# Block-sparse attention with a softplus FFN: the turned attention rows move one piece later, and the first key loads change queue

## The chip, the cores and the metric

One core of one Trainium2 chip runs the whole program. The metric is the device time of one execution in microseconds. Before the change three runs gave 786.46, 788.22 and 792.05 us; the median is 788.22 us.

## The reference

Attention over 4 batches of 8 heads, 768 positions in 24 blocks of 32, head size 64, float32. A query block sees its own block and both neighbours, the first and the last block, and three sampled blocks; the first and last query blocks see everything. Then a feed-forward layer on 3072 rows of 512, with 2048 hidden columns.

```python
scores = scale * np.matmul(q, k.transpose(0, 1, 3, 2))
mask = np.abs(blk_i - blk_j) <= window
mask = mask | (blk_i == 0) | (blk_j == 0) | (blk_i == n_blocks - 1) | (blk_j == n_blocks - 1)
...
attn = attn / (np.sum(attn, axis=-1, keepdims=True) + 1e-09)
...
h = x @ w_in
g = np.maximum(h, 0.0) + np.log1p(np.exp(-np.abs(h)))
return (g @ w_out).astype(np.float32)
```

## The kernel before

**Sets and units.** The 88 inner query blocks go in 22 sets ("s") of four; four more sets ("w") hold the first and last query blocks. A set has two units, each with half of the heads. For a unit, `scores` (L577) multiplies queries `qc` by gathered keys `kg` into PSUM tiles `s`; VectorE adds the mask and takes the maximum (L602, tile `pr`); `exponents` (L636) is ScalarE's exponential (L651), which also sums rows into `sums`; `transposes` (L655) turns `pr` on TensorE into PSUM tile `t` (L664), which ScalarE (L669) or VectorE (L667) copies to `pt`; `values` (L674) multiplies `pt` by the gathered values `vg` into PSUM tile `x` (L700).

**The end of a set.** `normalise` (L721) divides on VectorE: L731 and L732 invert the sums, L733 writes `xs`. `turn` (L753) transposes `xs` on TensorE into a PSUM tile `y` (L759, four matmuls); `x_high` (L770) copies it on ScalarE (L772), `x_low` (L774) takes the remainder on VectorE (L776). Both parts go into `X`, the FFN's input for three sets ("a tile", 8 in all).

**FFN, first part.** For each of 8 tiles and 6 of 16 column blocks, `hidden` (L255, tile `h`, 12 matmuls) and, three steps later, `project` (L318, tile `o`, 9 matmuls). The other ten column blocks come after attention, in a second part from about 440 us on (L1093 to L1215). Weights are converted on ScalarE and VectorE in small ticks between these (L181 to L231, tiles `raw`, `wt`, `w`).

**Who goes when.** `pieces` (L783) cuts attention into pieces. For an "s" set m the first holds its scores, the values and `normalise` of the set before; the second and third hold the transposes of its two units, with `turned_` (turn and `x_high`) and `lowered` (`x_low`) of the set before. `between` (L939) is called in the middle of `hidden`, between the products of `project` and after half steps, and runs the pieces due by then, so that FFN products stand between them. A tile's `hidden` may only be written after the third piece of its last set. In blocks under `manual_schedule`, and for SyncE everywhere, an engine follows program order. Elsewhere the framework's planner gives each engine its order from program order and from modelled costs; a later instruction may be put ahead of one that is not ready in the model. On the chip each engine then keeps that order. PSUM has four banks for `s`, `t`, `h` and `y` together (L126), and a bank is taken again once its readers are done.

**The start.** L403 loads a table of sampled blocks, broadcast to 128 partitions, from ScalarE's queue; `make_index` (L418) makes from it the rows that POOL gathers (L563). L406 loads the same blocks plain, for the registers that address key copies. Keys of batch 0 (`kT`) come in two loads, blocks 0 to 10 from SyncE and 11 to 23 from ScalarE. `gather_keys` (L500) fills `kg`: a copy of three neighbours for all four blocks (L515), the first and last block (L524), and three sampled blocks for each (L537). For the first set these copies are on VectorE and ScalarE. Meanwhile L860 keeps TensorE running with products that nobody reads (`warm`).

Of the kernel before, what the change touches and what calls it, by code (L numbers as in the profile page):

```python
# [10 lines left out]
I32 = mybir.dt.int32  # L11
# [25 lines left out]

PARK = 8

WARM = 41  # L40

AHEAD = 0.5

# [11 lines left out]
def sparse_attention_ffn(  # L55
# [344 lines left out]
                    nc.vector.memset(mask[i * BLOCK : (i + 1) * BLOCK, j, slot : slot + 1], NEG)  # L400

    def load_blocks():
        nc.scalar.dma_start(  # L403
            out=table, in_=picks.bitcast(I32).unsqueeze(1).to_broadcast([NI, BLOCK, 2 * NW])
        )
        nc.sync.dma_start(out=plain, in_=blocks.bitcast(I32).rearrange("a b -> (a b)").unsqueeze(0))  # L406

    def pack_blocks():

# [14 lines left out]
                out=ix[:, b], in0=rx, scalar1=float(BLOCK), scalar2=iof[:, b : b + 1], op0=ALU.mult, op1=ALU.add  # L424
            )

    def make_mask():

        nc.vector.tensor_tensor(
            out=tmp, in0=rp, in1=iuf.unsqueeze(2).to_broadcast([P, PG, NR]), op=ALU.subtract  # L430
        )
        nc.vector.tensor_tensor(out=tmp, in0=tmp, in1=tmp, op=ALU.mult)
        nc.vector.tensor_single_scalar(out=hit, in_=tmp, scalar=1.0, op=ALU.is_le)
        for end in (0.0, float(LAST)):
            nc.vector.scalar_tensor_tensor(
                out=hit, in0=rp, scalar=end, in1=hit, op0=ALU.is_equal, op1=ALU.max
            )
        for s in range(1, NR):

            n = NR - s  # L440
            nc.vector.tensor_tensor(out=tmp[:, :, 0:n], in0=rp[:, :, s:NR], in1=rp[:, :, 0:n], op=ALU.is_equal)
            nc.vector.tensor_tensor(out=hit[:, :, s:NR], in0=hit[:, :, s:NR], in1=tmp[:, :, 0:n], op=ALU.max)
        nc.vector.tensor_single_scalar(out=mask[:, :, 4 : 4 + NR], in_=hit, scalar=NEG, op=ALU.mult)
# [56 lines left out]
    def gather_keys(j, b, lo, hi):  # L500
        kd = kg[j % 2]
        blk0 = group[j][lo][1]

        stale = [i for i in range(lo, hi) if ended_in.get((j % 2, i)) != b]
        for i in stale:
            ended_in[j % 2, i] = b

        def of_block(i):

            eng = (nc.vector if i < 2 else nc.scalar) if j == 0 else nc.gpsimd  # L510
            copy = nc.scalar.copy if j == 0 and i >= 2 else eng.tensor_copy
            if i == lo:
                at = kT[b][:, blk0 - 1 : blk0 - 1 + NR, :]
                pattern = [list(x) for x in at.ap]
                ins = nc.vector.tensor_copy(  # L515
                    out=kd[:, lo:hi, 0:NR, :].rearrange("p i s f -> p i (s f)"),
                    in_=bass.AP(at.tensor, at.offset, [pattern[0], [NP * BLOCK, hi - lo], [1, NR * NP * BLOCK]]),
                )
                tc.keep_in_program_order(ins)
                if stale:  # L520
                    rows = slice(stale[0], stale[-1] + 1)
                    first = nc.vector.tensor_copy if j == 0 else nc.scalar.copy
                    for end, slot, blkno in ((first, NR, 0), (nc.scalar.copy, 2 * NR + 1, LAST)):
                        ins = end(  # L524
                            out=kd[:, rows, slot, :],
                            in_=kT[b][:, blkno : blkno + 1, :].to_broadcast([P, len(stale), NP * BLOCK]),
                        )
                        if j:
                            tc.keep_in_program_order(ins)
            blk = group[j][i][1] - 1  # L530
            (r,) = registers(eng, [blk // 2])
            for s in range(NR):
                x = nc.s_assert_within(
                    eng.snap((r >> (16 * (blk % 2) + 5 * s)) & 31), 0, LAST,
                    skip_runtime_bounds_check_because="a sampled block is one of the key blocks",
                )
                copy(  # L537
                    out=kd[:, i, 1 + NR + s, :], in_=kT[b][:, bass.ds(x, 1), :].rearrange("p n f -> p (n f)")
                )

        key_work.extend((j, lambda i=i: of_block(i)) for i in range(lo, hi))


# [239 lines left out]
    def pieces():  # L783

        out = []

        def piece(*fs, wide=False):
            out.append((fs, wide))

        def scored(n):  # L790
            scores(n)
            m, a = units[n]
            what, j = sets[m]
            if a < NA - 1:
                return
            if what == "s":
                load_keys(j + 2)
            elif j + 1 < B:

                gathered(key_work, NM)  # L800
                for part in (0, 3, 1, 2):
                    load_kT(j + 1, part)
                waiting.append(BEHIND)

        def valued(n):
            values(n)
            m, a = units[n]
            if a == NA - 1:
                load_values(m + 2)

        def turned_(m):
            if turns_now(m):
                turn(m)
                x_high(m)

        def lowered(m):
            if turns_now(m):
                x_low(m)

        piece((transposes, 1))  # L820
        for m in range(1, len(sets) + 1):
            u, before = 2 * m, m - 1
            kind = sets[m][0] if m < len(sets) else None
            whole = sets[before][0] == "w"
            if whole:
                piece((valued, u - 2), (transposes, u - 1))
            gone = [(valued, u - 1)] if whole else [(valued, u - 2), (valued, u - 1)]
            if kind == "s":
                piece((scored, u), (scored, u + 1), *gone, (load_queries, m + 2), (exponents, u), (normalise, before), wide=True)
                piece((exponents, u + 1), (turned_, before), (transposes, u))  # L830
                piece((lowered, before), (transposes, u + 1))
            elif kind == "w":
                piece((scored, u), (exponents, u))
                piece((scored, u + 1), *gone, (load_queries, m + 2), (exponents, u + 1), (normalise, before))
                piece((turned_, before), (transposes, u))
                out[-1] = (out[-1][0] + ((lowered, before),), False)
            else:
                piece(*gone, (normalise, before))
                piece((turned_, before))
                piece((lowered, before))  # L840
            ready[before] = len(out)
        return out
# [8 lines left out]
    weights = Weights(early + later, 3, 4)  # L851

    load_blocks()
    load_queries(0)

    load_part(0, 0, FIRST, nc.sync)
    load_part(0, FIRST, NB, nc.scalar)
    warm = ps_s.tile([P, 4, P], F32, tag="s", name="warm")
    for n in range(WARM):
        nc.tensor.matmul(warm[:, n % 4], ident, ident, start=True, stop=True)  # L860
    with tc.manual_schedule(engines={mybir.EngineType.DVE}):
        make_index()
        pack_blocks()
        make_mask()
        load_keys(0)
        gathered(key_work, 0)
    load_queries(1)
    load_values(0)
    load_keys(1)
# [584 lines left out]
```

## Time and profile before

| what | value |
|---|---|
| median of three runs | 788.22 us |
| the profiled execution | 791.96 us, span 790.2 us |
| TensorE busy | 740.5 us, 94% of the span |
| VectorE busy | 591.9 us, 75% |
| ScalarE busy | 556.5 us, 70% |
| GpSimd (POOL) busy | 270.1 us, 34% |
| mean granted TensorE clock | 0.981 |

The span runs from the first to the last instruction; 1.8 us of the execution lie around it. PE is TensorE's matmul row, PEld its weight loads, DVE VectorE, ACT ScalarE, POOL GpSimd, SP SyncE. Matmul records overlap, since matmuls are pipelined, so the start of the next record says more than the length of one. A float32 product counts as two records, a transpose as one.

### The profile page before, as it was taken

The numbers are of one execution on the slowest core, as the hardware profiler recorded it, in microseconds if no ns is written. First come the engines' busy times: TensorE is split into PE (matmuls) and PEld (weight loads), VectorE is DVE, ScalarE is ACT, GpSimd is POOL, SyncE is SP. The second block draws the span as 40 slices with busy tenths as digits, with TensorE's granted clock in tenths as the row PEclk, the third lists the DMA queues.
The fourth block names the chain that finished last, engine by engine and source line by source line (L and its number), as shares of the span: only waits on it lengthen the run. The fifth ranks groups of instructions, "written<-read, shape, count | busy, mean of one in ns | idle before, by whom it ended". The sixth has DMA issues, their size and how long they took to land.

```text
span 790.2 us, 21936 instructions
## 1 busy us (share of the span) xinstructions
PE 740.5 (94%) x8350; PEld 628.5 (80%) x8350; DVE 591.9 (75%) x1446; ACT 556.5 (70%) x1297; POOL 270.1 (34%) x446
## 2 busy tenths in 40 slices
PE   8888898899888998998999998999999999999997
PEld 7556677778777777876788977898999998989996
DVE  5689998767867867775567975677786676777865
ACT  4678987767867777777577868766667666676663
POOL 7744545315333153442010036862503413310000
PEclk9899999999999998999999999999999999999999
DMA  8788865949747698447554624302331132120301
GB/s 307 258 289 337 318 255 190 338 162 377 261 165 260 219 359 293 149 136 280 189 193 159 223 85 149 107 30 79 108 107 52 56 107 98 42 76 1 107 1 54
DMA packets 54336, 137.81 MB, mean 174 GB/s; under 512 B 5781, under 2 KB 18582, under 8 KB 50518
## 3 DMA queue, kind: packets, MB, share of 16 engines
q1 hardware_dynamic: 46466, 111.49, 40.0%
q0 software_dynamic: 7120, 23.34, 7.8%
q8 instruction: 66, 1.08, 0.5%
q10 hardware_dynamic: 644, 1.57, 0.5%
q14 instruction: 40, 0.33, 0.1%
HBM read 105.97 MB, written 30.41 MB: 173 GB/s over the span
## 4 chain that ended last, share of the span: by engine, by line
PE 69%; ACT 13%; DVE 10%; issue 3%; DMA 2%; POOL 1%; SPq 0%; POOLq 0%; ACTq 0%; DVEq 0%
PE o L1213 6%; PE o L1214 6%; PE o L1215 6%; ACT pr L651 5%; PE t L664 5%; PE a L1101 3%; PE a L1103 3%; PE a L1102 3%; PE s L596 3%; PE h L263 3%; PE h L264 3%; PE h L265 3%; PE o L327 3%; PE o L328 3%; PE o L329 3%
## 5 line engine op out<-in xcount | busy, mean ns | idle before, releaser
L563 POOL DMA_INDIRECT vg<-in_v_dram,ix x88 | 94.0, 1068 | 116.7 <-PE x L700 90.7
L651 ACT ACTIVATE pr<-pr,nmax 128x256 f32<-128x256 f32 (+1 forms) x192 | 101.8, 532 | 28.3 <-DVE nmax L602 22.8
L537 POOL COPY kg<-kT 128x128 f32 x252 | 71.7, 324 | 110.7 <-PE s L596 104.5
L1213 PE MATMUL o<-w,gh 128*128 128x512 f32 x240 | 94.4, 393 | 0.0
L1214 PE MATMUL o<-w,gh 128*128 128x512 f32 x240 | 94.3, 393 | 0.0
L1215 PE MATMUL o<-w,gl 128*128 128x512 f32 x240 | 94.0, 392 | 0.0
L1188 ACT CAST gh<-a 128x512 fp32r<-128x512 f32 x30 | 17.6, 587 | 79.1 <-DVE a L1184 79.1
L263 PE MATMUL h<-x,w 128*128 128x384 f32 x192 | 70.2, 366 | 3.2 <-issue 1.9
L602 DVE CUSTOM_DVE_ANT_1 pr<-s,mask 128x256 f32<-128x256 f32 x176 | 62.8, 421 | 8.6 <-PE s L596 8.4
L264 PE MATMUL h<-x,w 128*128 128x384 f32 x192 | 66.0, 344 | 0.0
L664 PE MATMUL t<-ident,pr 128*128 128x128 f32 x448 | 63.9, 289 | 2.2 <-ACT pr L651 0.9
L265 PE MATMUL h<-x,w 128*128 128x384 f32 x192 | 65.7, 342 | 0.0
L664 PEld LDWEIGHTS t<-ident,pr 128*128 128x128 f32 x448 | 54.2, 148 | 8.8 <-issue 2.3
L700 PEld LDWEIGHTS x<-vg,pt 128*32 128x32 f32 x2816 | 42.1, 110 | 22.9 <-issue 21.7
L327 PE MATMUL o<-w,gh 128*128 128x512 f32 x144 | 59.2, 411 | 0.0
L329 PE MATMUL o<-w,gl 128*128 128x512 f32 x144 | 57.5, 399 | 0.0
L328 PE MATMUL o<-w,gh 128*128 128x512 f32 x144 | 57.3, 398 | 0.0
L700 PE MATMUL x<-vg,pt 128*32 128x64 f32 x2816 | 48.4, 221 | 8.5 <-issue 8.5
L596 PE MATMUL s<-kg,qc 64*32 64x256 f32 x1408 | 54.3, 397 | 2.0 <-DVE pt L667 0.7
L1215 PEld LDWEIGHTS o<-w,gl 128*128 128x128 f32 x240 | 45.1, 188 | 10.1
L669 ACT COPY pt<-t 128x512 f32<-128x512 f32 x82 | 45.8, 585 | 9.5 <-PE t L664 5.3
L1172 DVE SCALAR_TENSOR_TENSOR b<-b,e 128x512 f32<-128x512 f32 x30 | 20.9, 698 | 39.9 <-ACT l L1168 39.9
(206 smaller groups left out, 2160.5 us busy)
## 6 DMA issues: line engine op xcount, KB each, us to landing
vg<-in_near_dram SPq DMA_DIRECT2D x21, 1024.0 KB
xD<-x SPq DMA_DIRECT2D x8, 1536.0 KB
raw<-in_w_in_dram SPq DMA_DIRECT2D x16, 512.0 KB
raw<-in_w_out_dram SPq DMA_DIRECT2D x16, 512.0 KB
q<-xD SPq DMA_DIRECT2D x16, 512.0 KB
vg<-in_v_dram SPq DMA_DIRECT2D x12, 512.0 KB
yD<-os SPq DMA_DIRECT2D x24, 256.0 KB
y<-yD SPq DMA_DIRECT2D x24, 256.0 KB
```

What stands on the lines that cost most here:

```text
L263: nc.tensor.matmul(out_, wh[:, cols], hi, start=(c == 0), stop=False)
L264: nc.tensor.matmul(out_, wh[:, cols], lo, start=False, stop=False)
L265: nc.tensor.matmul(out_, wl[:, cols], hi, start=False, stop=(c == NC - 1))
L327: nc.tensor.matmul(po[m], gh[:, cols], wh, start=first, stop=False)
L329: nc.tensor.matmul(po[m], gl[:, cols], wh, start=False, stop=last)
L563: nc.gpsimd.indirect_dma_start(out=vd[:, 1, i, :], out_offset=None, in_=v, in_offset=bass.IndirectOffsetOnAxis(ap=ix[:, b, blk_ : blk_ + 1 ...
L651: nc.scalar.activation(x, x, AF.Exp, bias=nmax[:, r, j : j + 1], scale=-1.0, accum_out=rs[:, h : h + 1])
L664: nc.tensor.transpose(ps[:, i], st["pr"][r][:, c * P : (c + 1) * P], ident)
L700: nc.tensor.matmul(xq[rows, h * D : (h + 1) * D], pt[r, 2 * j + c][:, rows], vd[:, c, i, h * D : (h + 1) * D], start=(c == 0), stop=(c == 1),)
L1213: nc.tensor.matmul(po[m], gh[:, cols], wh, start=first, stop=False)
L1214: nc.tensor.matmul(po[m], gh[:, cols], wl, start=False, stop=False)
L1215: nc.tensor.matmul(po[m], gl[:, cols], wh, start=False, stop=last)
```

## The change

1. In an "s" set, `turned_` of the set before leaves the second piece and goes to the head of the third, ahead of the second unit's transposes; `lowered` goes behind them. "w" sets keep their order.
2. At the start SyncE issues the table, then both loads of keys, then the first queries; ScalarE issues the plain blocks alone. Before, SyncE issued plain blocks, queries, first keys, and ScalarE the table and the second keys.
3. The first set's copy of three neighbours moves from VectorE to ScalarE and, with the copies of the end blocks, ahead of the first part of the mask (`near_mask`); the second part (`twice_mask`) comes behind VectorE's copies of sampled blocks.
4. 28 warm products instead of 41.

```diff
-WARM = 41
+WARM = 28
...
-        nc.scalar.dma_start(
+        nc.sync.dma_start(
             out=table, in_=picks.bitcast(I32).unsqueeze(1).to_broadcast([NI, BLOCK, 2 * NW])
         )
-        nc.sync.dma_start(out=plain, in_=blocks.bitcast(I32).rearrange("a b -> (a b)").unsqueeze(0))
+        nc.scalar.dma_start(out=plain, in_=blocks.bitcast(I32).rearrange("a b -> (a b)").unsqueeze(0))
...
+        def beside():
+
+            at = kT[b][:, blk0 - 1 : blk0 - 1 + NR, :]
+            pattern = [list(x) for x in at.ap]
+            ins = (nc.vector.tensor_copy if j else nc.scalar.copy)(
+                out=kd[:, lo:hi, 0:NR, :].rearrange("p i s f -> p i (s f)"),
+                in_=bass.AP(at.tensor, at.offset, [pattern[0], [NP * BLOCK, hi - lo], [1, NR * NP * BLOCK]]),
+            )
+            tc.keep_in_program_order(ins)
...
+                    if j or slot > NR:
+                        tc.keep_in_program_order(ins)
...
+            if i == lo and j:
+                beside()
...
+        if j == 0:
+            key_work.append((j, beside))
...
-                piece((exponents, u + 1), (turned_, before), (transposes, u))
-                piece((lowered, before), (transposes, u + 1))
+                piece((exponents, u + 1), (transposes, u))
+                piece((turned_, before), (transposes, u + 1), (lowered, before))
...
     load_blocks()
+    load_part(0, 0, FIRST, nc.sync)
+    load_part(0, FIRST, NB, nc.sync)
     load_queries(0)
-
-    load_part(0, 0, FIRST, nc.sync)
-    load_part(0, FIRST, NB, nc.scalar)
...
         make_index()
         pack_blocks()
-        make_mask()
         load_keys(0)
+        key_work.pop(0)[1]()
+        near_mask()
         gathered(key_work, 0)
+        twice_mask()
```

## Rows read from the trace of the kernel before

**Rows 1.** The page's head and its first part: span, then busy time of each engine, share of the span, instructions.

```profile
span 790.2 us, 21936 instructions
PE 740.5 (94%) x8350; PEld 628.5 (80%) x8350; DVE 591.9 (75%) x1446; ACT 556.5 (70%) x1297; POOL 270.1 (34%) x446
```

**Rows 2.** Busy time by stretch: the stretch in us, its length, then busy time and instructions of PE, PEld, DVE, ACT and POOL, the granted TensorE clock (1.00 is 2.4 GHz), the DMA engines' share and GB/s.

```profile
56.00:110.00 54.00, 48.59 (x842) 36.37 (x842) 51.50 (x145) 46.93 (x122) 27.17 (x56) 0.97 0.86 327
110.00:440.00 330.00, 305.57 (x4608) 254.48 (x4607) 246.97 (x678) 243.97 (x614) 103.34 (x213) 0.97 0.65 234
440.00:790.00 350.00, 340.50 (x2087) 304.18 (x2085) 254.10 (x488) 230.70 (x465) 100.78 (x84) 1.00 0.24 78
```

**Rows 3.** Waits of PE from 110 to 440 us: line, what ended the wait, then us in total, times, the longest.

```profile
PE y L759 <- DVE xs L733: 16.1, 9, 2.3
PE x L700 <- issue: 3.2, 3, 1.9
...
PE y L759 <- DVE wt L212: 1.9, 1, 1.9
```

**Rows 4.** The same view from 20 to 56 us, and (second row) from 56 to 110 us.

```profile
PE y L759 <- DVE xs L733: 3.9, 3, 1.6
...
PE y L759 <- DVE xs L733: 0.9, 1, 0.9
```

**Rows 5.** PE in order of time, one set from its scores to the next set's: start, duration, engine, line, operation, operands, count, and in brackets the idle time before with its releaser.

```profile
219.15 1.96 PE L596 MATMUL s<-kg,qc 64*32 64x256 f32 x64
...
223.93 0.34 PE L265 MATMUL h<-x,w 128*128 128x384 f32 x1
226.58 0.65 PE L759 MATMUL y<-ident,xs 128*128 128x128 f32 x4 [2.31 <-DVE xs L733]
...
228.67 0.52 PE L264 MATMUL h<-x,w 128*128 128x384 f32 x1
...
232.67 1.04 PE L664 MATMUL t<-ident,pr 128*128 128x128 f32 x8
...
237.82 1.96 PE L596 MATMUL s<-kg,qc 64*32 64x256 f32 x64
```

**Rows 6.** The same set on ACT (the fourth of eight exponentials, and the end of the eighth) and on DVE.

```profile
222.97 0.49 ACT L651 ACTIVATE pr<-pr,nmax 128x256 f32<-128x256 f32 x1
...
225.34 0.18 ACT L651 ACTIVATION_READ_ACCUMULATOR pr<-pr,nmax 128x1 f32 x1
225.56 0.17 DVE L731 TENSOR_SCALAR sums<-sums 128x8 f32<-128x8 f32 x1 [1.71 <-ACT pr L651]
...
225.88 0.64 DVE L733 TENSOR_TENSOR xs<-x,sums 128x512 f32<-128x512 f32 x1
...
227.88 0.69 DVE L776 TENSOR_TENSOR x<-y,x 128x512 fp32r<-128x512 f32 x1 [0.49 <-ACT x L772]
```

**Rows 7.** The last such wait of the stretch: ACT's fourth exponential of the set, and PE's wait.

```profile
372.41 0.49 ACT L651 ACTIVATE pr<-pr,nmax 128x256 f32<-128x256 f32 x1
...
376.02 0.66 PE L759 MATMUL y<-ident,xs 128*128 128x128 f32 x4 [2.30 <-DVE xs L733]
```

**Rows 8.** Busy time by stretch, as in rows 2: the wait of rows 5 and what follows it, then two more stretches at the low clock.

```profile
224.27:226.58 2.31, 0.00 (x1) 0.01 (x1) 0.99 (x4) 1.25 (x6) 1.54 (x4) 1.00 0.83 326
227.60:230.80 3.20, 3.20 (x13) 3.10 (x12) 2.84 (x5) 1.55 (x4) 2.14 (x2) 0.50 1.03 409
...
309.50:316.20 6.70, 5.85 (x22) 5.46 (x23) 4.27 (x9) 3.28 (x8) 2.44 (x3) 0.50 0.89 345
340.20:343.50 3.30, 3.30 (x15) 3.30 (x16) 2.37 (x5) 1.76 (x6) 2.41 (x3) 0.50 0.99 350
```

**Rows 9.** PE at the start, in order of time: the last 17 warm records, both units' scores, and the first values.

```profile
10.80 2.06 PE L860 MATMUL warm<-ident 128*128 128x128 f32 x17
12.79 2.03 PE L596 MATMUL s<-kg,qc 64*32 64x256 f32 x64
...
18.02 0.30 PE L700 MATMUL x<-vg,pt 128*32 128x64 f32 x2 [0.55 <-issue]
19.40 0.42 PE L700 MATMUL x<-vg,pt 128*32 128x64 f32 x2 [1.08 <-issue]
```

**Rows 10.** The other engines at the start: the table's issue, its user, ACT's and DVE's key copies, POOL's fourth gather of values.

```profile
0.78 1.20 ACTq L403 DMA_DIRECT2D xe<-in_picks_dram  x1
5.49 0.72 DVE L423 TENSOR_SCALAR ix<-xe,iof 128x24 int32<-128x24 int32 x4 [1.83 <-DMA xe<-in_picks_dram]
...
10.21 0.95 POOL L563 DMA_INDIRECT vg<-in_v_dram,ix  x1 [0.30 <-issue]
10.38 0.62 ACT L524 COPY kg<-kT 128x512 f32<-128x512 f32 x1 [8.35 <-DMA kT<-in_k_dram]
11.39 1.45 ACT L537 COPY kg<-kT 128x128 f32 x6 [0.40 <-DVE kg L537]
```

**Rows 11.** DMA queues from 12 to 14 us: packets, MB, share of 16 engines (q1 is SyncE's, q0 POOL's).

```profile
q1 hardware_dynamic: 95, 0.58, 71.9%
q0 software_dynamic: 88, 0.27, 34.5%
```

**Rows 12.** The last turn before the FFN's first tile, and VectorE's remainder of it.

```profile
51.63 0.65 PE L759 MATMUL y<-ident,xs 128*128 128x128 f32 x4 [0.82 <-DVE xs L733]
...
54.54 0.68 DVE L776 TENSOR_TENSOR x<-y,x 128x512 fp32r<-128x512 f32 x1
```

More of the change, by code (lines that the diff above doesn't have):

```diff
@@ L425, in make_index, with near_mask @@
             )
-    def make_mask():
+    def near_mask():
         nc.vector.tensor_tensor(
@@ L437, in make_mask, with twice_mask @@
             )
+    def twice_mask():
         for s in range(1, NR):
@@ L506, in gather_keys @@
             ended_in[j % 2, i] = b
+        def beside():
[6 more added lines that the diff above has]
+            tc.keep_in_program_order(ins)
+            if stale:
+                rows = slice(stale[0], stale[-1] + 1)
+                first = nc.vector.tensor_copy if j == 0 else nc.scalar.copy
+                for end, slot, blkno in ((first, NR, 0), (nc.scalar.copy, 2 * NR + 1, LAST)):
+                    ins = end(
+                        out=kd[:, rows, slot, :],
+                        in_=kT[b][:, blkno : blkno + 1, :].to_broadcast([P, len(stale), NP * BLOCK]),
+                    )
+                    if j or slot > NR:
+                        tc.keep_in_program_order(ins)
         def of_block(i):
@@ L511, in of_block @@
             copy = nc.scalar.copy if j == 0 and i >= 2 else eng.tensor_copy
[L512 to L529, printed above, removed]
+            if i == lo and j:
+                beside()
             blk = group[j][i][1] - 1
@@ L834, in pieces @@
                 piece((scored, u + 1), *gone, (load_queries, m + 2), (exponents, u + 1), (normalise, before))
-                piece((turned_, before), (transposes, u))
-                out[-1] = (out[-1][0] + ((lowered, before),), False)
+                piece((turned_, before), (transposes, u), (lowered, before))
             else:
```

## The prediction

> **What bounds the kernel now.** I read the page's busy shares first: TensorE works 94% of the span, nobody else over 75% [rows 1]. Then busy time by stretch. From 440 us on TensorE has 340.5 of 350 us, and the change touches nothing there. From 110 to 440 us it has 305.6 of 330, so 24.4 us are idle, while VectorE and ScalarE are busy 75% and 74%. From 56 to 110 us VectorE is busy 51.5 of 54 us: that stretch is VectorE's [rows 2]. Then PE's waits: of the 24.4 us, 16.1 and 1.9 are one wait, ten times over, that of the turn `y` for `xs`; the next one is 3.2 us [rows 3]. Nothing stands beside it: in one such case PE has no work for 2.31 us [rows 5, 8].
>
> Why is `xs` late? In that set scores begin at 219.15 and `hidden`'s first half ends at 224.27. L731, which inverts the sums of a later set, stands ahead of L733 on VectorE and waits until the eighth exponential is read out at 225.52; then L733 ends at 226.52 and `y` starts [rows 5, 6]. PE, in order, holds the first unit's transposes behind `y`. These need only the unit's own four exponentials, and those ended at 223.46, 0.8 us before PE came.
>
> **Part 1, the turn one piece later.** No instruction is added or removed. In the usual set PE goes scores, values, half a `hidden`, [wait], `y`, t(u), half a `hidden`, nine products, t(u+1). After the change t(u) follows the half `hidden` at once, and `y` stands about 5 us later by the same rows (232.67 less 226.58, less the 0.5 of `y` itself), where `xs` has long been written. So a wait goes whole if the first four exponentials have ended by then. The last of the ten reads the same: they ended at 372.90, and PE came at 376.02 less 2.30, 373.72 [rows 7]. At most 18.0 us are won; at worst nothing, if VectorE or ScalarE is late by as much at the next place. ScalarE's copies of t(u) then stand behind the last exponentials, and the other engines' 75% become 79% of a stretch 18 us shorter (247.0 of 312). I take 15.0, five sixths, because no other wait of PE for VectorE or ScalarE in this stretch comes near these [rows 3].
>
> What is late next? `y` holds one of four PSUM banks until `x_low` is done: 226.58 to 228.57, 2.0 us [rows 5, 6]. Behind the new place come t(u+1), a `hidden` and nine products, 5.15 us until the next scores (232.67 to 237.82), so the cover holds. `x_low` also feeds the next tile's `hidden`; before the first tile it took from 51.63 to 55.22, 3.6 us [rows 12], and there the first `hidden` follows the transposes directly. Of the 3.9 us of the three waits from 20 to 56 us [rows 4] I therefore take 0.5: this stretch ends with that tile and hands over to a stretch that VectorE fills. The bounds are 0 and 3.9. The 0.9 us from 56 to 110 lie in a "w" set, whose order stays: 0.
>
> **The clock.** After the wait of rows 5, in which TensorE did nothing, the granted clock was 0.50 (1.2 GHz) from 227.6 to 230.8, and the same work took 0.52 in place of 0.34 us a record. The low clock also stands at 340.2 and, for 6.7 us, at 309.5 [rows 5, 8]. Work there would take half the time: 13.2 us at half speed cost 6.6 at most. Three low stretches beside ten waits leave seven waits that brought none, and without these waits other places may bring some; I take 1.7, one stretch of 3.3 us. The bounds are 0 and 6.6. The Trainium skill, "TensorE: Matmul & The Clock Gate", section "What's actually happening", has it that the throttled state is the default and activity releases it. By that rule all three stretches should go, and the sum would be 4.9 us lower; the trace agrees in part, since seven waits brought no fall. The rule speaks against the 13 warm products taken away, too.
>
> **Part 2, the start.** Twenty-six warm records at 0.12 us each (2.06 over 17) are 3.1 us, so warm ends near 9.8 instead of 12.8 [rows 9]. The keys decide next: ScalarE saw the second load at 10.38 and was done with its copies at 12.84 [rows 10], 2.5 us later. Two loads of queries (128 x 512 floats, 0.26 MB each) no longer go ahead of K or beside it: at 0.85 MB in 2 us [rows 11] that is 1.2 us, and up to 0.8 more for loads of values that used to run beside it. The table's issue took 1.20 us on ScalarE [rows 10]; on SyncE it stands ahead of K and can cost K all of that. SyncE's later issues (second queries, near values) come later by that and by one issue of K; ScalarE has one short issue left. Scores so begin 0 to 2 us sooner; I take 1.2. The neighbours' copy, now on ScalarE (three times the 0.62 us of a 512-wide one, at most 1.9 us) fits between the two key loads; the mask's second part, five operations on at most 33 columns, runs behind VectorE's copies while the scores take 2.03 us [rows 9], and would show whole only if it outlasted them.
>
> But the set cannot go on: the first values wait until 19.40, 1.08 us after 0.55 us before, labelled issue [rows 9]. Their transposes are long there; what they still need is the fourth gather, issued by POOL at 10.21 [rows 10]. The gathers depend on the table (its first user ran at 5.49, after 1.83 us of waiting) and on the DMA engines, which are full: q0 moved 0.27 MB in 2 us, so one gather of 256 KB takes 1.9 us [rows 11]. Sooner keys do not move that. I take 0.5 us for an earlier table; the bounds are 3.1 won (warm's share whole) and 1.2 lost (the longer SyncE queue).
>
> The Trainium skill, "DMA: Bandwidth & Descriptors", section "Queues, rings and completion order", says that each DMA engine takes turns between queues packet by packet. The trace agrees (95 packets against 88, though 0.58 MB against 0.27). By it the gathers would meet one rival queue instead of two while K loads, and the sum would be up to 1 us lower by an estimate from that page; no row shows it.
>
> **Sum.** 15.0 + 0.5 + 1.7 + 0.5 = 17.7 us. The profiled execution took 791.96 us (790.2 of span and 1.8 around it) and would become 774.3; it is the slow end of three, 3.7 above their median. I set the sum against the median: 788.2 less 17.7 is 770.5.
>
> **Rivals.** *The wait moves on* (0.22): PE, freed of `y`, meets t(u+1), the copies or a full VectorE, and half comes back. For it: VectorE was 2.3 us late with `xs` in this very place [rows 5]. Against: the exponentials in rows 5 to 7 were in time. 9 of 18 us won, nothing else: 779.2; a quarter won: 783.7.
>
> *The clock follows as well* (0.06): by the skill's rule above all three low stretches go. In rows: 18.0 + 6.6 off the median gives 763.6.
>
> *The edit does not do what it says* (0.07): the planner may put `y`, ready in its model, ahead of a t(u) that is not, and the order stays. Against: at `y`'s new place half a `hidden` and nine products, ready on the chip, would have to be passed over too. Only the start's 0.5 us is left: 787.7.
>
> *The turned bank stops the next scores* (0.09), the side of a loss: `y` now holds its bank up to the scores. `x_low` lags `y` by 2.0 us in the middle and 3.6 before the first tile; the scores come 5.15 + 0.5 us behind `y`. From a lag of 5.65 on each set pays the excess; at 5.65 + 18/16 = 6.8 us in all 16 sets of this stretch the gain is eaten. At 7.5 us it costs 16 x 1.85 = 30 less 18, so 800. Nothing in the rows comes near that lag, hence the small chance.
>
> **How the numbers follow.** The forecast has 0.56. A measurement of this kernel can tell about 1%, 7.9 us. Faster than 780.3: the forecast, the clock case and half of the second case, 0.56 + 0.06 + 0.10 = 0.72, less 0.01 for the forecast's own upper end: 0.71. Slower than 796.1: 0.08 of the bank case. The rest, 0.21, is within 1%. The forecast's own range is 765 to 777: 18 us against 12 for the waits, 0 to 6.6 for the clock, the start from 1.2 lost to 2 won. The range stretches to the second case, whose upper end is 783.7, and down to the clock case: 763 to 784 leaves out the case without effect and the bank case, 0.16, and tails.
>
> **What would show it.** Right: PE's waits of `y` for `xs` from 110 to 440 us fall from 18.0 to under 2 us; TensorE is busy 97% or more there; t(u) starts with no wait behind half a `hidden`. The first scores start at 10.8 to 12.8, and the first values still wait until about 19 us. Wrong: waits of t for `pr`, of s for `x_low`, of `y` itself as long as before, or a low clock in stretches that had none.

## The result, and the profile after

The changed kernel takes 764.74 us (median of 6 runs, 764.14 to 767.85) beside 789.28 us for the kernel before (6 runs, 786.46 to 792.05): a ratio of 0.9701, with a 95% interval of 0.967 to 0.9732, so 24.5 us less. The profiled execution took 764.14 us, with a span of 762.4. In the rows of after, line numbers behind the edits have moved: the turn is L768 (before L759), the inverted sums L740 (L731), `xs` L742 (L733), transposes L673 (L664), scores L605 (L596), values L709 (L700), warm L867 (L860).

The page's head and first part, which answers to [rows 1]:

```profile
span 762.4 us, 21888 instructions
PE 729.2 (96%) x8324; PEld 620.8 (81%) x8324; DVE 588.5 (77%) x1445; ACT 555.5 (73%) x1298; POOL 273.3 (36%) x446
```

TensorE has 26 records fewer (the 13 warm products) and its share rose from 94% to 96%. Busy time by stretch, as in [rows 2]; attention now ends 28 us sooner, so the second stretch is read to 420:

```profile
56.00:110.00 54.00, 48.63 (x832) 37.28 (x831) 51.74 (x146) 48.53 (x124) 27.93 (x56) 0.97 0.84 317
110.00:420.00 310.00, 303.03 (x4638) 253.18 (x4637) 252.08 (x692) 245.74 (x625) 105.43 (x212) 1.00 0.69 249
```

The first row is that of before, nearly to the digit: VectorE fills that stretch in both. Nothing is won there: PE's work of 60.86 us in the kernel before starts 2.9 us sooner in the kernel after, that of 111.26 us 2.2 us sooner. In the second TensorE is busy 97.8% in place of 92.6%, and the granted clock has gone from 0.97 to 1.00. PE's waits from 110 to 440 us, beside [rows 3]:

```profile
PE h L263 <- DVE u L276: 2.9, 2, 1.5
PE x L709 <- issue: 1.0, 1, 1.0
PE y L768 <- DVE xs L742: 0.7, 1, 0.7
PE t L673 <- DVE pt L676: 0.7, 1, 0.7
```

The ten waits of `y` were 18.0 us and are one of 0.7. PE in order of time, the same set as in [rows 5]:

```profile
215.42 0.34 PE L265 MATMUL h<-x,w 128*128 128x384 f32 x1
215.60 1.04 PE L673 MATMUL t<-ident,pr 128*128 128x128 f32 x8
216.39 0.42 PE L263 MATMUL h<-x,w 128*128 128x384 f32 x1
...
219.61 0.60 PE L768 MATMUL y<-ident,xs 128*128 128x128 f32 x4
220.05 1.21 PE L673 MATMUL t<-ident,pr 128*128 128x128 f32 x8
222.72 0.44 PE L263 MATMUL h<-x,w 128*128 128x384 f32 x1 [1.46 <-DVE u L276]
```

The transposes start 0.18 us behind the half `hidden`, with no bracket: nothing was waited for. `y` comes 4.0 us later. VectorE in the same set, beside [rows 6]:

```profile
218.09 0.17 DVE L740 TENSOR_SCALAR sums<-sums 128x8 f32<-128x8 f32 x1 [1.71 <-ACT pr L660]
...
218.42 0.64 DVE L742 TENSOR_TENSOR xs<-x,sums 128x512 f32<-128x512 f32 x1
...
222.12 0.55 DVE L276 SCALAR_TENSOR_TENSOR u<-h,e 128x384 f32<-128x384 f32 x1
```

VectorE still stands for the same 1.71 us before L740. The change did not take VectorE's wait away; it took PE out of its way, and what is left of it shows two steps later, where `u` is late and `hidden` waits 1.46 us. (That the one comes of the other is tried below, with the order kept.) At the start, PE in order of time, beside [rows 9]:

```profile
7.80 2.96 PE L867 MATMUL warm<-ident 128*128 128x128 f32 x25
10.88 3.14 PE L605 MATMUL s<-kg,qc 64*32 64x256 f32 x64
...
16.26 0.42 PE L709 MATMUL x<-vg,pt 128*32 128x64 f32 x12
18.10 0.91 PE L709 MATMUL x<-vg,pt 128*32 128x64 f32 x4 [1.43 <-DMA vg<-in_v_dram,ix]
```

Scores begin 1.9 us sooner; the last of the first values still wait for their gather. The table reads the traces at fixed points of the work: the start of the first scores, of the first `hidden` of tiles 0, 1 and 7, of the second part, and the end (us). The profile of the kernel before is near the slow end of its runs, that of the kernel after is its fastest run, and that of "after, 41 warm" (777.34 us) is the slowest of six with a median of 773.87, so the columns differ by more than the medians do. "Idle" is the time between tile 1 and tile 7 that no PE record covers, "low" the time there at a granted clock of 0.50, and "values" PE's waits for values labelled issue, from 56 to 180 us. The middle columns belong to experiments below.

| | before | start alone | move alone | after, 41 warm | move, 28 warm | after | after, order kept |
|---|---|---|---|---|---|---|---|
| scores | 12.8 | 11.8 | 12.3 | 13.7 | 11.2 | 10.9 | 11.3 |
| tile 0 | 54.2 | 52.6 | 53.7 | 55.8 | 52.8 | 52.5 | 51.3 |
| tile 1 | 120.3 | 117.6 | 120.8 | 125.5 | 117.6 | 117.4 | 116.2 |
| tile 7 | 430.6 | 426.2 | 410.1 | 415.8 | 402.6 | 402.6 | 400.1 |
| second part | 445.3 | 440.9 | 424.8 | 430.5 | 417.3 | 417.3 | 414.8 |
| end | 790.2 | 785.7 | 770.0 | 775.5 | 762.4 | 762.4 | 759.7 |
| idle | 23.5 | 23.6 | 9.0 | 9.0 | 6.6 | 6.9 | 5.7 |
| low | 17.0 | 13.6 | 3.4 | 6.8 | 0 | 0 | 0 |
| values | 5.0 | 1.5 | 7.3 | 8.5 | 0.8 | 0.8 | 0.6 |

Between the two profiles the span fell by 27.8 us: 2.9 by tile 1, 25.1 from tile 1 to tile 7, nothing after it. Of the 25.1, idle time makes 16.6, and 17.0 us of low clock that are gone make 8.5 if that work ran at half speed.

### The profile page after: what moved, and what is told of

Its sections match the earlier page's. It is cut to its first block, busy times and chain, and to the rows that moved or that the text cites. A ratio compares the mean times of both kernels' runs of the same rounds, so it can differ in the third digit from the quotient of the medians.

```text
span 762.4 us, 21888 instructions
## 1 busy us (share of the span) xinstructions
PE 729.2 (96%) x8324; PEld 620.8 (81%) x8324; DVE 588.5 (77%) x1445; ACT 555.5 (73%) x1298; POOL 273.3 (36%) x446
## 4 chain that ended last, share of the span: by engine, by line
PE 61%; ACT 17%; DVE 12%; issue 4%; DMA 3%; POOL 2%; POOLq 0%; ACTq 0%; DVEq 0%
PE o L1222 7%; PE o L1223 7%; PE o L1224 7%; ACT pr L660 5%; PE a L1110 3%; PE a L1112 3%; PE a L1111 3%; PE h L263 3%; PE t L673 3%; PE x L709 3%; PE b L1111 2%; PE b L1110 2%; PE b L1112 2%; PE h L264 2%; PE h L265 2%
## 5 line engine op out<-in xcount | busy, mean ns | idle before, releaser
L544 POOL COPY kg<-kT 128x128 f32 x252 | 73.4, 333 | 90.7 <-PE s L605 82.9
L263 PE MATMUL h<-x,w 128*128 128x384 f32 x192 | 69.6, 362 | 4.7 <-DVE u L276 2.9
L673 PE MATMUL t<-ident,pr 128*128 128x128 f32 x448 | 62.9, 283 | 3.4 <-DVE pt L676 1.1
L264 PE MATMUL h<-x,w 128*128 128x384 f32 x192 | 64.7, 337 | 0.6 <-issue 0.6
L265 PE MATMUL h<-x,w 128*128 128x384 f32 x192 | 64.6, 337 | 0.0
L673 PEld LDWEIGHTS t<-ident,pr 128*128 128x128 f32 x448 | 52.3, 144 | 10.0 <-ACT pr L660 3.2
L709 PEld LDWEIGHTS x<-vg,pt 128*32 128x32 f32 x2816 | 42.1, 110 | 22.3 <-issue 18.3
L709 PE MATMUL x<-vg,pt 128*32 128x64 f32 x2816 | 48.1, 221 | 8.4 <-issue 6.9
L605 PE MATMUL s<-kg,qc 64*32 64x256 f32 x1408 | 51.1, 394 | 0.6 <-DVE u L276 0.3
```

The lines of the kernel that those rows point to most:

```text
L263: nc.tensor.matmul(out_, wh[:, cols], hi, start=(c == 0), stop=False)
L264: nc.tensor.matmul(out_, wh[:, cols], lo, start=False, stop=False)
L265: nc.tensor.matmul(out_, wl[:, cols], hi, start=False, stop=(c == NC - 1))
L544: copy(out=kd[:, i, 1 + NR + s, :], in_=kT[b][:, bass.ds(x, 1), :].rearrange("p n f -> p (n f)"))
L673: nc.tensor.transpose(ps[:, i], st["pr"][r][:, c * P : (c + 1) * P], ident)
L709: nc.tensor.matmul(xq[rows, h * D : (h + 1) * D], pt[r, 2 * j + c][:, rows], vd[:, c, i, h * D : (h + 1) * D], start=(c == 0), stop=(c == 1),)
```

## Experiments

**The two parts by themselves.** Each kernel has one of the two.

The kernel before with the turn moved:

```diff
-                piece((exponents, u + 1), (turned_, before), (transposes, u))
-                piece((lowered, before), (transposes, u + 1))
+                piece((exponents, u + 1), (transposes, u))
+                piece((turned_, before), (transposes, u + 1), (lowered, before))
```

> Only the turn moves; the start stays as before (41 warm products, loads and copies as before). Theory: the move carries nearly all of the gain, since the start's 2 us are used up in the stretch that VectorE fills (56 to 110 us): 765 to 768 us, against 764.7 with both and 789.3 before; waits of y for xs from 110 to 440 us under 2 us. Rival: the start gives its 2 us or more to the end, or the low clock was a matter of chance: 770 us or above.

The kernel after with the pieces of before:

```diff
-                piece((exponents, u + 1), (transposes, u))
-                piece((turned_, before), (transposes, u + 1), (lowered, before))
+                piece((exponents, u + 1), (turned_, before), (transposes, u))
+                piece((lowered, before), (transposes, u + 1))
```

> Only the start changes (28 warm products, loads, copies, mask in two parts); the turn stays in the second piece. Theory: first scores near 10.9 us as after, first hidden about 1 to 2 us sooner, and at the second tile's first hidden (120 us) the lead is under 1 us; the time 788 to 790 us, not to be told from before. Rival: the lead lasts: 786.5 us or less, 2 us or more under before.

The move alone took 772.0 us (769.7 to 775.1), ratio 0.9762 [0.9728, 0.9797]; the start alone 786.65 (782.4 to 788.7), ratio 0.9932 [0.9901, 0.9963]. Their product is 0.9696, so the parts add up to the whole change, and both of my expectations were off on the same side: the start gives more than half a microsecond, and its lead is not eaten by the waits behind it. PE's waits from 110 to 440 us in the start alone:

```profile
PE y L768 <- DVE xs L742: 22.8, 11, 3.1
```

So with the start alone the waits of `y` grow by 4.8 us over [rows 3], while those for values in the table fall by 3.5: a wait taken away ahead of a longer one in the same set passes to it in large part. Set by set: in the kernel before, values wait at 120.06, 136.27 and 154.52 us (0.87, 0.42, 1.94 us) and the `y` behind them 0.76, 1.27 and not at all; with the start alone those values do not wait, and `y` waits 1.87, 1.89 and 1.21. With the move alone it is the values that wait:

```profile
PE x L700 <- issue: 5.5, 4, 2.9
PE h L263 <- DVE u L276: 1.5, 1, 1.5
```

**Which piece of the start it is.** The start has two pieces: other queues and key copies, and 13 warm products less. First the kernel after with the 41 products back:

```diff
-WARM = 28
+WARM = 41
```

> The changed kernel with 41 warm products again, so that the first scores cannot start before 12.3 us (10.9 with 28). Theory: the first values still wait for the fourth gather until about 18.6 us, so the lead at the first hidden shrinks by under 0.7 us: the time within 1 us of the changed kernel. Rival: the lead comes from the scores' start: 1.4 us or more slower.

It took 773.87 us (771.6 to 777.3) beside 766.56 (765.7 to 770.4) for the kernel after, run again with it on the same chip: 7.3 us. The expectation of at most 1 us fell. Then the kernel with the move alone and 28 products, loads and key copies as before:

```diff
-WARM = 41
+WARM = 28
```

> Kernel before with the turn moved and 28 warm products, the start's loads and key copies as before. Asked: is the start's part of the gain owned by the shorter warm alone, or does it need keys that land sooner? Theory (both are needed): the second key load is still seen by ScalarE at about 10.4 us and its last copy still ends at about 12.8, so the first scores begin at 12.5 to 12.8 though TensorE is free at 9.8; the first hidden of tile 0 comes at 53.5 to 54.5 and the time is 770 to 774, within 2 us of the kernel with the move alone (772.0). Rival (warm's length is all): scores begin under 11.8, tile 0 at 52.5 or sooner, time 764 to 768. A third way: the idle time between warm and scores brings a low clock over the first scores, and the time is over 774.

It took 764.61 us (764.2 to 768.5), ratio 0.9706 [0.967, 0.9742], and the rival held but for tile 0 (52.8, where it wanted 52.5 or sooner): the shorter warm alone gives the whole of the start's gain. New queues and copies gave nothing that shows: 0.9706 without and 0.9701 with them at 28 products, 0.9762 and 0.9777 at 41. PE at its start:

```profile
5.67 5.00 PE L860 MATMUL warm<-ident 128*128 128x128 f32 x37
11.20 0.62 PE L596 MATMUL s<-kg,qc 64*32 64x256 f32 x4 [0.54 <-ACT kg L524]
12.07 2.68 PE L596 MATMUL s<-kg,qc 64*32 64x256 f32 x60 [0.25 <-DVE kg L537]
...
18.58 0.30 PE L700 MATMUL x<-vg,pt 128*32 128x64 f32 x2 [1.18 <-DMA vg<-in_v_dram,ix]
```

The scores do not wait for the last key copy. They begin 0.5 us behind the warm products and run along with the copies, waiting 0.54 and 0.25 us for them. So in the kernel before it was the warm products that held the start of the scores, not the keys. Their end is another matter. PE in the kernel with the move alone, which has 41 products:

```profile
12.34 2.54 PE L596 MATMUL s<-kg,qc 64*32 64x256 f32 x64
...
19.44 0.42 PE L700 MATMUL x<-vg,pt 128*32 128x64 f32 x2 [0.25 <-DMA vg<-in_v_dram,ix]
```

The scores end at 14.88 us there and at 14.75 with 28 products; the first sixteen records of values end at 19.86 and, with 28, at 20.06. The 1.1 us by which the scores begin sooner are used up by then, as the prediction had said.

So what is won later is not that lead carried on. It comes anew: 0.9 us at tile 0, 3.2 at tile 1, 7.5 at tile 7. Where it comes from is mostly in the table's last line, PE's waits for values, and a little in the line above it. From 56 to 180 us, first in the kernel with the move alone:

```profile
PE x L700 <- issue: 7.3, 5, 2.9
```

then in the one with the move and 28 products:

```profile
PE x L700 <- issue: 0.8, 1, 0.8
```

The four waits that go are these, PE in the kernel with the move alone:

```profile
104.00 0.32 PE L700 MATMUL x<-vg,pt 128*32 128x64 f32 x8 [1.70 <-issue]
...
120.56 0.33 PE L700 MATMUL x<-vg,pt 128*32 128x64 f32 x9 [0.94 <-issue]
...
136.43 0.33 PE L700 MATMUL x<-vg,pt 128*32 128x64 f32 x9 [0.55 <-issue]
...
154.12 0.33 PE L700 MATMUL x<-vg,pt 128*32 128x64 f32 x9 [2.89 <-issue]
```

Of the 128 records of a set's values the last eight or nine stand still. "Issue" means that the trace shows no event that released them; what they lack by position is the last gather, as at the start, where another such wait is labelled with the gather. Each of the six profiles with 41 products has five waits of values in that stretch, 5.0 to 8.5 us in sum; each of the eight with 28 has one, 0.6 to 2.1 us. PE, VectorE, ScalarE and POOL run the same instructions in the same order in both kernels, from the first scores to the end, so it is not another order but a matter of when things meet. A chain that would do it can be read from POOL: its gathers for a set wait until PE is done with the values of two sets before, in the kernel with the move alone:

```profile
91.85 1.31 POOL L563 DMA_INDIRECT vg<-in_v_dram,ix  x1 [0.47 <-PE x L700]
```

Late values give the next gathers a late start, and those make the next values late. That 13 products more bring these waits is shown, with the old start (772.0 against 764.61) and with the new (773.87 against 766.56); the chain is argued, and I did not try it alone.

**Is it the DMA engines that the first gather lacks?** The kernel after, with one load of neighbouring values put later:

```diff
-    load_values(1)
     load_keys(2)
     scores(1)
     exponents(0)
     load_queries(2)
+    load_values(1)
```

> Kernel after with the second set's load of neighbouring values (SyncE, 0.5 MB, issued at about 4.3 us) put behind the third load of queries, which SyncE issues at about 14 us, and POOL's gathers for that set in the same place of the program. Asked: does the first set's fourth gather, for which the values waited 1.43 us until 18.10, land later because the DMA engines are shared? Theory (it does): with 0.5 MB less beside it, about 1.2 us at the 0.85 MB that two queues moved in 2 us, the values' wait for the gather falls under 0.7 us and the first of them starts by 17.2; tile 0's first hidden comes up to 1 us sooner. The time stays within 2 us of the kernel after (764.7 to 766.6), since the load has to be made later all the same. Rival (the gather's own descriptors or its place in POOL's queue set its landing): the wait stays over 1.1 us.

PE at its start:

```profile
11.84 2.26 PE L605 MATMUL s<-kg,qc 64*32 64x256 f32 x64 [1.57 <-DMA qc<-in_q_dram]
...
16.34 0.43 PE L709 MATMUL x<-vg,pt 128*32 128x64 f32 x16
```

All 16 records run in one piece, where they waited 1.43 us for the gather in the kernel after, and POOL issues that gather at 9.21 us here and at 9.20 there: it lands sooner with the load out of its way, and the theory held. Tile 0 starts at 50.7 in place of 52.5, more than the 1 us expected, although this time the scores waited 1.57 us for queries; at tile 7 only 0.5 us of this are left (402.1 against 402.6). The time, 762.42 us (759.8 to 763.6), is 0.3 us below the range given; its ratio of 0.9658 [0.9613, 0.9703] overlaps that of the kernel after, so no gain in time is shown.

**Does filling the pauses keep the clock, and is it worth it?** The kernel before, with products that nobody reads ahead of the ten turns that waited, 64 in all:

```diff
+    FILL = {6: 3, 7: 4, 11: 6, 12: 8, 13: 8, 14: 7, 16: 5, 18: 7, 19: 8, 20: 8}
...
+        for n in range(FILL.get(len(turns_done), 0)):
+            nc.tensor.matmul(ps[:, n % NP], ident, ident, start=True, stop=True)
+        turns_done.append(m)
```

> The kernel before, with 3 to 8 extra products of ident with itself ahead of the ten turns that waited between 110 and 440 us, sized to 85% of each wait and written where the turn writes afterwards; the output is unchanged. No wait is taken away, TensorE only works through most of it. Theory: TensorE's idle time brings the low clock: the low stretches of 227.6, 309.5 and 340.2 us go, and with them 4 to 7 us: 782 to 786 us. Rival: the low clock there was chance, or the transposes and scores bring it: low stretches of 10 us or more stay between 110 and 440 us, and the time is 789 us within 2.

It took 789.53 us, ratio 0.9988 [0.9964, 1.0012]: no gain. PE around the turn of [rows 5]:

```profile
225.52 1.95 PE L761 MATMUL y<-ident 128*128 128x128 f32 x16
227.99 0.66 PE L764 MATMUL y<-ident,xs 128*128 128x128 f32 x4 [0.53 <-DVE xs L733]
```

and two stretches, the whole and the one that follows this turn:

```profile
110.00:440.00 330.00, 317.16 (x4751) 266.94 (x4750) 249.30 (x685) 246.74 (x619) 106.18 (x213) 0.99 0.65 235
...
226.00:230.00 4.00, 3.48 (x30) 3.29 (x29) 2.49 (x6) 2.25 (x7) 2.93 (x4) 1.00 0.94 350
```

The clock part held: where [rows 8] has 0.50 behind the pause it is 1.00 now, and of 17.0 us of low clock from tile 1 to tile 7 only 3.4 are left. The time part missed. From tile 1 to tile 7 it takes 307.1 us in place of 310.3. Idle time falls from 23.5 to 11.6, the clock's share by 6.8, and the 64 products (128 records) cost 15.9 (0.25 each): 11.9 and 6.8 less 15.9 would be 2.8 won; 3.2 were measured in this profile, and 1.1 of them had been lost ahead of tile 1. The runs give the clock's share without the luck of one profile: their mean granted clock has a median of 0.990 (12 runs) against 0.985 for the kernel before beside them (19 runs), which is at most 4 us of 789. With that, 11.9 and 4 are just what the products cost. Busy is not the same as useful.

The kernel before once more, for a second profile:

> The kernel before once more, for a second profile. Theory (a pause of TensorE before a low stretch is what brings it, but not each pause brings one): the ten waits of y stand in the same places within 0.5 us each, 17 to 19 us in sum, and the low clock again covers 10 to 20 us from 110 to 440, not at all the same places as in the first profile. Rival (the low stretches belong to fixed places of the program): the same three stretches, at 227.5, 309.5 and 340.2 us after shifts of the start are taken off, and no other.

It took 787.35 us. The waits of `y` are 16.2 us, ten times (17 to 19 expected; two of them are over 0.5 us shorter than before). The low clock from 110 to 440 us covers two stretches:

```profile
226.70:230.00 3.30, 3.30 (x16) 3.30 (x15) 2.35 (x5) 1.76 (x3) 2.44 (x3) 0.50 1.01 390
308.70:312.00 3.30, 3.30 (x16) 3.30 (x15) 2.61 (x6) 1.74 (x3) 2.24 (x2) 0.50 1.01 394
```

Both stand where two of the three of [rows 8] did; at the third place PE waited 1.91 us for `xs` in both profiles, and only in the first did the clock fall. A fourth low stretch of the first profile, 3.4 us from 155.8 us on, is not in [rows 8]; it stands behind a wait of 1.94 us for values, and the second profile has the same wait there and no fall. The numbers I had given (10 to 20 us, other places) missed with 6.8 us, and so did the rival's "the same three". What is common to these stretches is the pause ahead: 2.31 us (both profiles of before), 1.93 and the first part of 1.27 (the first profile, before 309.5), 2.09 and 0.53 (the second, before 308.7), 2.89 (the move alone, before 154.9). But waits of 2.33 and 2.30 us for `xs` (358.93 and 376.02 in the first profile, 2.33 and 2.31 in the second) brought no fall in either. The kernel after has no pause over 1.5 us from 110 to 440 and no low clock there.

**Is VectorE's hoisted instruction the root?** In [rows 6] L731, of a later set, stands ahead of L733. The kernel before and the kernel after, each with the three instructions of `normalise` held in program order:

```diff
-        nc.vector.tensor_scalar_add(out=rs, in0=rs, scalar1=1e-9)
-        nc.vector.reciprocal(out=rs, in_=rs)
-        nc.vector.tensor_tensor(
+        tc.keep_in_program_order(nc.vector.tensor_scalar_add(out=rs, in0=rs, scalar1=1e-9))
+        tc.keep_in_program_order(nc.vector.reciprocal(out=rs, in_=rs))
+        tc.keep_in_program_order(nc.vector.tensor_tensor(
```

> The kernel before, with the three instructions of normalise held in program order on VectorE, so that the next set's sums cannot be inverted ahead of xs. Theory: in part of the ten waits L731 of a later set, waiting for the last exponentials, is what makes xs late; waits of y for xs fall from 18 to 6 to 12 us and the time to 778 to 784 us. Rival: VectorE's queue is late by itself; the waits stay at 15 us or more and the time within 2 us of 789.

On the kernel before it gave 784.42 us, ratio 0.9897 [0.9852, 0.9942], and the waits of `y` became

```profile
PE y L759 <- DVE xs L733: 13.3, 9, 2.2
```

a little over the 12 us that I had put as the upper end, as the time is over the 784; so the hoisting is a part of the 18.0 us (16.2 in the second profile) and not all of them. Moving the turn does more.

> The changed kernel with normalise held in program order on VectorE. Theory: xs is early enough now, so its order gives nothing: within 1.5 us of the changed kernel. Rival: the sums of a later set block VectorE for other work too (before the change, holding the order won about 6 us while the waits of y fell by only 4.7): 3 us or more faster than the changed kernel.

On the kernel after it gave 761.32 us (760.6 to 763.2), ratio 0.9628 [0.9594, 0.9662]: 5.2 us less than the kernel after beside it on the same chip, and faster than both kernels of this case. My expectation of at most 1.5 us fell. VectorE in the set of the rows above:

```profile
214.71 0.17 DVE L740 TENSOR_SCALAR sums<-sums 128x8 f32<-128x8 f32 x1
...
215.22 0.69 DVE L742 TENSOR_TENSOR xs<-x,sums 128x512 f32<-128x512 f32 x1
...
219.11 0.54 DVE L276 SCALAR_TENSOR_TENSOR u<-h,e 128x384 f32<-128x384 f32 x1
```

L740 has no bracket now, `u` is 3.0 us sooner (0.9 of them because the whole tile begins sooner), `hidden` follows the transposes without a wait, and tile 3 takes 46.8 us in place of 49.3; so the 1.71 us stop was what made `u` late. Tile 4 gives 1.0 of this back (54.8 against 53.8). Beside the second profile of the kernel after, on the same chip, the lead is 2.0 us at tile 0, 3.1 at tile 1 and 4.9 at tile 7; what makes the part before tile 1 I did not take apart.

**Smaller ones.** The turn behind the second unit's transposes:

```diff
-                piece((turned_, before), (transposes, u + 1), (lowered, before))
+                piece((transposes, u + 1), (turned_, before), (lowered, before))
```

> The changed kernel with the turn one place later still, behind the second unit's transposes. Theory: there is little left to win (0.7 us of such waits from 110 to 440 us), and the cover of the PSUM bank, 5.65 us, shrinks by 1 us and still holds: within 2 us of the changed kernel. Rival, the turned bank: scores or hidden wait for x_low, 3 us or more slower than the changed kernel.

768.02 us (766.9 to 771.7) beside 766.56: the place within the piece does not matter, and the later release of the bank stops nobody. The kernel after once more, beside it:

> The changed kernel itself once more, beside the next three on one chip, and for a second profile. Theory: its time is steadier than that of the kernel before, because TensorE's idle time there brings the low clock in some stretches and not in others: 764 to 768 us, and no low clock from 110 us to the end but for the last few us. Rival: the low clock is chance: a stretch or two of 3.4 us at half speed between 110 and 400 us.

766.56 us, ratio 0.9707 [0.9668, 0.9746]. The theory held: its profile has no low clock from 110 to 440 us. Its six runs lie within 4.7 us, eleven of the kernel before beside it within 9.2 (786.8 to 796.0). Each run's mean granted clock shows that the low clock comes in some executions more than in others: 0.987 to 0.996 in the six, where the two slowest runs have the two lowest, and 0.979 to 0.991 in the eleven, where the slowest has the lowest. And the two edits that had moved something, together (order kept, neighbouring values later):

> Kernel after with both edits that had moved something: the three instructions of normalise kept in program order, and the second set's near values put behind the third queries. Theory (the two gains lie in different places, the one from tile 3 to tile 4 and in the waits of y before tile 0, the other in the first values' wait, so they add): ratio to the kernel before 0.956 to 0.962, 755 to 759, and tile 3 to tile 4 again takes 46.5 to 47.5 us. Rival (the start's 2 us and order's gain before tile 0 are the same microseconds): ratio 0.962 to 0.966.

761.01 us (759.2 to 763.7), ratio 0.9644 [0.961, 0.9678]: the rival's side. Tile 3 again takes 46.8 us, but tile 0 begins at 53.0 in its profile. The first values again run in one piece (15.95 to 16.38), yet the later load adds nothing that shows on top of the order kept (0.9628 [0.9594, 0.9662]).

## Why the prediction was right, and what in it was not

**Faster, by the mechanism given.** PE's wait for `xs` was on the path, and PE had other work in hand. The marks I had set are met: 0.7 us of these waits (under 2), TensorE busy 97.8% (97 or more), transposes without a wait in the set shown, scores at 10.88 (10.8 to 12.8; in the second profile of the kernel after 9.63, below that), first values held until 18.10 (about 19).

**The waits.** 15.0 us were taken. With the move alone the idle time from tile 1 to tile 7 falls by 14.5 (23.5 to 9.0). The three microseconds I had held back for a late next place are there too: 2.9 us of `hidden` for `u` in two waits, one of them (1.46) from the same 1.71 us stop of VectorE that I had read in [rows 6]. I had asked what PE meets next, but not what the stop itself, still standing, would make late.

**The clock.** 1.7 taken, 6.8 measured with the move alone (13.6 us of low clock gone), which is over my bound of 6.6. That bound was short: I had counted three low stretches, 13.2 us, where the trace has a fourth from 155.8 us on, 17.0 in all. Against the second profile of before it is 1.7 only (6.8 us low in that one, 3.4 in the move alone): the size depends on which execution one has, and a single profile does not give it. The runs do: the mean granted clock has a median of 0.985 in 19 runs of the kernel before (0.975 to 0.994) and of 0.992 in the six of the move alone (0.990 to 0.994). What is missing to 1.00, times the span, is 11.8 us and 6.2, so the clock is worth up to 5.6 us of the 18.6 that the move won, an estimate, since a wait during a low stretch costs nothing more. The term was too small by a factor of about three. The Trainium skill, "TensorE: Matmul & The Clock Gate", section "What's actually happening", by which activity releases the throttle, led to the case in which all three stretches go. The traces agree in part: the three went and none took their place in the kernel after, and with 64 idle products in the pauses they went as well; but pauses of up to 2.33 us brought no fall in two profiles of before.

**Before tile 0.** 0.5 taken; with the move alone tile 0 starts at 53.7 in place of 54.2.

**The start is the term that failed.** The prediction had: "Sooner keys do not move that. I take 0.5 us". The first values did wait, as said, and the new loads moved nothing, as said; with the move alone the first values even end at the same time with 41 and with 28 products (19.86 and 20.06). But I took that wait as a floor under all that follows, and the warm products as hidden. Measured: 7.3 us for the 13 products (773.87 against 766.56). Two readings were wrong. "The keys decide next" holds for the end of the scores alone; for their start it overlooked that the scores of the first pairs need only some of the copies, and follow the others as they come. And what I had costed at most at 3.1 us, the warm products' own time, is worth more, since later waits come or go with it: the 3.2 us of values in [rows 3] were in the rows I read, and I left them as fixed. Why they turn on the start stays open.

**The sum and the cases.** The move alone took 18.6 us off its median (790.57 to 772.0) against 17.2 forecast for it; the start alone took 5.4 us (0.9932 of 789.28) against 0.5. The 24.5 us won are 6.8 more than the 17.7 forecast, and about 5 of these are the start's. The result is 0.3 us below the 765 to 777 that I gave as the forecast's own range; 763 to 784 holds it only because I had stretched it to the case of the clock, and that is luck. The case of the clock stood at 763.6, next to the result, but by 18.0 and 6.6 and no start, which the move alone, at 772.0, denies: that it stands so near is luck too. Of the other rivals, the wait that moves on was there in small (2.9 of 18 us, not 9); the edit did what it says; and the turned bank stopped no scores, not even with the turn later still.

## What to carry to other kernels

When an engine in order waits for a late result, look for work of its own behind the wait that is ready, and put the wait behind it; then follow the late engine itself, because its stop is still there and will show at its next customer. Work that only keeps an engine busy is not free at the start just because something else waits later: try its length by itself. And a gain that is won by filling a pause with idle work was spent on that work here (15.9 us for 11.9 of idle time and about 4 of clock); reorder useful work into it instead.

## What the runs showed that I had not expected

- Thirteen products of 0.24 us (26 records of 0.12) at the very start decide whether the values of sets 80 to 140 us later wait, by position for their gathers: 5.0 to 8.5 us in five places with them, 0.6 to 2.1 in one without, in every profile of this case. Why is not settled; a lead of the first sets is not needed for it, since in one pair it is gone at the first values.
- The granted clock fell to 0.50 (1.2 GHz) after pauses of TensorE of 1.9 to 2.9 us, at some places in two profiles of the same kernel, but not after each: one of 1.91 us for `xs` brought it in the first and not in the second. In both profiles of the kernel after it fell once between tile 0 and tile 1 (82.4 and 83.6 us), where only 0.90 and 0.56 us of pauses went ahead, so a long pause is not the only way to it.
- Putting key loads on another queue, and the copies on another engine, changed the time by less than can be measured here (0.9706 and 0.9701), though the keys were seen 0.8 us sooner (ScalarE's copy at 9.60 against 10.38 [rows 10]).
